# Unit 0 of a fused gated-recurrence and feed-forward kernel: stacking issued from two queues, its four score groups ahead of its outputs, its transposes and state updates last

## The chip, the cores and the metric

The kernel runs on one core of a Trainium2 chip. The metric is the time of one execution in device microseconds (us), as the median of the runs shown: 691.08 us over three runs (691.05 to 691.49).

## What is computed

The reference runs a gated linear recurrence over the sequence and feeds its output to a feed-forward layer. There are 4 batches, 8 heads, 768 tokens and 48 values to a head; the state is a complex 48x48 matrix for each batch and head.

```python
mag = np.sqrt(a_re * a_re + a_im * a_im)
scale = np.minimum(mag, 0.999) / (mag + 1e-06)
...
for t in range(S):
    new_re = ar * S_re - ai * S_im
    new_im = ar * S_im + ai * S_re
    S_re, S_im = (new_re + kv, new_im)          # kv = outer(k_t, v_t)
    y[:, :, t] = np.einsum('bhd,bhde->bhe', q[:, :, t], S_re)
...
x = attn_out.transpose(0, 2, 1, 3).reshape(B * S, H * D)   # 3072 x 384
return ((x @ w_a) * (x @ w_b)) @ w_out                     # d_ff = 1536
```

## The kernel before

**Units.** The work is cut into 12 units: 2 pairs of batches by 6 chunks of 128 tokens. A unit has 256 columns (its two batches, i = 0 and 1). The recurrence over a chunk is turned into products of matrices: with the cumulative products of the gates, z, multiplied into q and divided out of k, the output of a chunk is a masked score matrix times v plus q times the state that came in, and the state is carried from chunk to chunk.

**Steps of a unit u.**

- prep(u), on DVE (VectorE) and ACT (ScalarE): the gates are normed (L178 to L193), the cumulative products are built (L211 and L213, then pairs of L227 and L233, then L289, L294, L297 to L305), and q and k are multiplied by them. The last two operations of prep(u) are the two multiplications L309 into the tile qk.
- stack(u), L338 to L347: ten DMAs from SBUF to SBUF bring the eight heads of qk into the tile stk, each head on partitions of its own. Two heads straddle a block of partitions and take two DMAs each. SP (SyncE) issues all of them in before. There is one stk and one qk, so the next load of q and k waits for the whole of stack.
- attn(u): scores(i, g), with g one of two groups of four heads: four matmuls into a tile pm on PE (TensorE, L379), then the multiplication by the causal mask into a tile am on DVE (L382). There are two am buffers. outputs(i): 16 matmuls of am and v into xp, and 16 more of q and the state except where a chunk begins a sequence (L422), then ACT casts xp to xh (L424). residual(i): xp minus xh, by a matmul with a negated identity on PE (L432) and a cast on ACT (L435) for units 0 and 1, on DVE for later units. transposes(i, g): four on PE (L390) and a copy to kt on ACT (L394). state(i, g): four matmuls of kt and v (L445), and then a copy into the state u on ACT where a chunk begins a sequence (L454) or an addition on DVE (L452).
- the feed-forward of unit u (its window): for each of 12 blocks f of the inner dimension gemm1 (L489, 18 matmuls), a copy h_t on ACT (L497), the product h_t on DVE (L498), a cast hh on ACT (L499), a difference hl on DVE (L500), and gemm2 (L507, six matmuls) two blocks later. After each unit its output is stored from ACT's queue (L647).

The matmuls work on pairs of a rounded number and its remainder, so the weights are split once at the start (split_weights): per piece three operations on DVE (L134, L136, L138), a cast (L142) and a copy (L149) on ACT, and two matmuls (L147, L148). Six blocks of the weights are split ahead of unit 0's attention, the others during window 0. A weight piece is called w, then m (0, 1 or 2: w_a, w_b, w_out), then f: w111 is w_b's block 11.

**What sets the order.** The program is written as one stream of steps. Unit 0's attention stands in front of window 0, with parts of prep(1) between its steps; the attention of unit w+1 is put between the blocks f of window w, and stack(w+2) and the load behind it follow at a fixed block of window w. Within a step, priorities move the DVE and ACT operations of attention and feed-forward ahead (ATTN_FIRST, MOE_FIRST), and a scheduler that runs when the program is built puts each engine's instructions into one fixed order. On the chip each engine then works its own list in that order and waits on semaphores. The pools that tie the engines: three buffers for ab (gemm1's output), two for pm, one for xp, two for am, two for kt.

**Unit 0's order** (L463 to L466) is a list of its own: the scores of batch 0, its outputs, the scores of batch 1, the residual of batch 0, outputs of batch 1, transposes of batch 0, and then the rest. The list of later units stands above it.

Of the kernel before, what the change touches and what calls it, by code (L numbers as in the profile page):

```python
# [8 lines left out]
F32 = mybir.dt.float32  # L9
# [58 lines left out]
def tile_kernel(ctx: ExitStack, tc: tile.TileContext, a_d, qk_d, v_d, w_d, qn_d, kn_d, vn_d, an_d, out_d):  # L68
    nc = tc.nc
    vec, act, pe, sync = nc.vector, nc.scalar, nc.tensor, nc.sync  # L70
# [8 lines left out]
    kvp = fast.enter_context(tc.tile_pool(name="kvp", bufs=2))  # L79
# [26 lines left out]
    stk = const.tile([128, H, RUN], F32, name="stk")  # L106
    nc.gpsimd.memset(stk[KS:128], 0.0)
    qk = const.tile([128, NJ, 2, RUN], F32, name="qk")
# [88 lines left out]
    def rescaled(c):  # L197
        return c % 2 == 1 and c + 1 < NCH
# [139 lines left out]
    def stack(u):  # L338
        n = RUN if rescaled(u % NCH) else 2 * TOK
        for h in range(H):  # L340
            r0 = h * D
            while r0 < (h + 1) * D:
                j, p = divmod(r0, 128)
                m = min((h + 1) * D - r0, 128 - p)
                d0 = 2 * (r0 - h * D)
                sync.dma_start(out=stk[d0:d0 + 2 * m, h, 0:n], in_=qk[p:p + m, j, :, 0:n])
                r0 += m  # L347


# [12 lines left out]
                          (3 * g + 2, [(2 * g, 32), (2 * g + 1, 64)])):  # L362
            quads[q % 4].append((q // 4, [(h, g * 128 + off) for h, off in pieces]))

    def attn(u, xh, xl):

        c = u % NCH
        last = c + 1 == NCH
# [2 lines left out]
        def cols(i):  # L371
            return slice(i * C, (i + 1) * C), slice(TOK + i * C, TOK + (i + 1) * C)

        def scores(i, hg):
            qs, ks = cols(i)
            sp = ps_m.tile([128, 4, 128], F32, name="pm")
            for h4 in range(4):
                h = hg * 4 + h4
                pe.matmul(out=sp[:, h4], lhsT=stk[:, h, ks], rhs=stk[:, h, qs], start=True, stop=True)  # L379
            am = kvp.tile([128, 512], F32, name="am", bufs=2).rearrange("p (h t) -> p h t", h=4)  # L380
            with tc.high_priority(offset=ATTN_FIRST):
                vec.tensor_tensor(out=am, in0=sp, in1=mask[:].unsqueeze(1).broadcast_to([128, 4, 128]),  # L382
                                  op=ALU.mult)
            ams[i, hg] = am
# [52 lines left out]
        def state(i, hg):  # L437
# [12 lines left out]
            with tc.high_priority(offset=ATTN_FIRST):  # L450
# [4 lines left out]
                if rescaled(c):  # L455
                    vec.tensor_tensor(out=uv, in0=uv, in1=sv, op=ALU.mult)

        order = [(scores, 0, 0), (scores, 0, 1), (transposes, 0, 0), (transposes, 0, 1),
                 (outputs, 0, 0), (scores, 1, 0), (residual, 0, 0), (state, 0, 0), (scores, 1, 1),
                 (state, 0, 1), (transposes, 1, 0), (transposes, 1, 1), (outputs, 1, 0),  # L460
                 (state, 1, 0), (residual, 1, 0), (state, 1, 1)]
        if u == 0:
            order = [(scores, 0, 0), (scores, 0, 1), (outputs, 0, 0), (scores, 1, 0), (scores, 1, 1),  # L463
                     (residual, 0, 0), (outputs, 1, 0), (transposes, 0, 0), (transposes, 0, 1),
                     (residual, 1, 0), (state, 0, 0), (state, 0, 1), (transposes, 1, 0), (transposes, 1, 1),
                     (state, 1, 0), (state, 1, 1)]  # L466
        for fn, i, g in order:
            if not (last and fn in (transposes, state)):
                fn(i, g)
# [5 lines left out]
    def new_x():  # L475
        return (moe.tile([128, NJ, TOK], F32, name="xh"), moe.tile([128, NJ, TOK], F32, name="xl"))
# [139 lines left out]
    def drain(gen, ns=None):  # L616
        if gen is None:
            return
        left = ns
        for cost in gen:  # L620
            if left is not None:
                left -= cost or 0
                if left <= 0:
                    return
# [6 lines left out]
    p1 = prep(1)  # L631
    for _ in range(CONV_FIRST):
        next(ws)
    x_cur = new_x()
    for _ in attn(0, *x_cur):
        drain(p1, P1_A)
    pend = []

# [11 lines left out]
    for w in range(NU):  # L650
# [42 lines left out]
        x_cur = x_nxt  # L693
# [74 lines left out]
```

## Time and profile before

| what | value |
|---|---|
| median of 3 runs | 691.08 us (691.05 to 691.49) |
| the profiled execution: its time | 690.18 us |
| its span on the core | 688.5 us |
| instructions in it | 14290 |
| mean granted clock of PE | 0.972 |
| HBM read, written | 39.32 MB, 4.72 MB |

The profile is one execution of its own; its time lies 0.9 us below the median, and 1.7 us of it lie outside the span. All start times below are microseconds from the span's start. A row of a timeline has the start, the time from the first start to the last end of the instructions in it, the engine, the line, the operation and its tiles, how many there are, and in brackets how long the engine stood idle before it and what ended that. Instructions overlap in an engine's pipeline, so the distance from one start to the next is what an instruction adds.

### The profile page before, as it was taken

To read this page: it belongs to the slowest core of one execution; us is meant where nothing else is said; L and a number is where in the kernel's file an instruction comes from. 1 tells how busy PE (TensorE), PEld (TensorE's weight loads), DVE (VectorE), ACT (ScalarE), POOL (GpSimd) and SP (SyncE) were. 2 spreads that over 40 slices of the span, in tenths; PEclk is the share of its full clock that TensorE was granted. 3 is DMA by queue.
4 is the path that set the end of the run, shared out by engine and by line. 5 is a ranking of instruction groups with operands and counts; after the bars stand their busy time and mean duration, and the time that the engine had idled before them with its cause. 6 is when DMAs were issued, how large, how long until landed. Compare 5 with 4: busy or idle time off the path is not lost.

```text
span 688.5 us, 14290 instructions
## 1 busy us (share of the span) xinstructions
PE 644.5 (94%) x5842; PEld 608.3 (88%) x5842; DVE 550.1 (80%) x1259; ACT 310.1 (45%) x622; POOL 5.6 (1%) x11
## 2 busy tenths in 40 slices
PE   3547999999999999999999999999999999999996
PEld 1214889899999999999999999999999999999996
DVE  6999899998989989999898898999989963233221
ACT  7357664735445346354363553635542332221221
POOL 3000000000000000000000000000000000000000
PEclk9676999999999999999999999999999999999999
DMA  8963301513314225043160440611500500400000
GB/s 321 402 268 95 121 1 44 143 54 87 115 39 139 63 78 145 16 136 104 29 194 2 122 117 3 178 60 62 155 24 18 153 24 18 108 24 2 24 1 28
DMA packets 30232, 63.94 MB, mean 93 GB/s; under 512 B 3664, under 2 KB 7248, under 8 KB 30160
## 3 DMA queue, kind: packets, MB, share of 16 engines
q1 hardware_dynamic: 26704, 58.23, 27.3%
q10 hardware_dynamic: 3456, 4.72, 1.9%
q8 instruction: 48, 0.79, 0.5%
q14 instruction: 24, 0.20, 0.1%
HBM read 39.32 MB, written 4.72 MB: 64 GB/s over the span
## 4 chain that ended last, share of the span: by engine, by line
PE 66%; DVE 25%; ACT 4%; DMA 2%; issue 2%; SPq 0%; DVEq 0%; ACTq 0%
PE ab L489 33%; PE o L507 16%; PE xp L422 5%; PE pm L379 4%; PE pm L445 3%; DVE a_t L289 3%; DVE qk L309 2%; PE pm L390 2%; DVE h_t L498 2%; DVE hl L500 2%; PE pm L147 1%; DVE z L294 1%; DVE pr L227 1%; DVE am L382 1%; DVE pb L262 1%
## 5 line engine op out<-in xcount | busy, mean ns | idle before, releaser
L489 PE MATMUL ab<-xh,w 128*128 128x256 f32 x1728 | 341.6, 286 | 0.0
L489 PEld LDWEIGHTS ab<-xh,w 128*128 128x128 f32 x1728 | 277.2, 189 | 1.7 <-issue 0.8
L489 PE MATMUL ab<-xl,w 128*128 128x256 f32 x864 | 245.5, 284 | 0.0
L489 PEld LDWEIGHTS ab<-xl,w 128*128 128x128 f32 x864 | 163.0, 189 | 0.6 <-issue 0.2
L507 PE MATMUL o<-w,hh 128*128 128x384 f32 x576 | 152.7, 343 | 0.0
L497 ACT COPY h_t<-ab 128x256 f32<-128x256 f32 x144 | 53.4, 371 | 163.4 <-PE ab L489 163.4
L498 DVE TENSOR_TENSOR h_t<-ab,h_t 128x256 f32<-128x256 f32 x144 | 60.4, 420 | 64.6 <-ACT h_t L497 64.3
L507 PEld LDWEIGHTS o<-w,hh 128*128 128x128 f32 x576 | 96.6, 188 | 1.1 <-issue 1.0
L507 PE MATMUL o<-w,hl 128*128 128x384 f32 x288 | 97.2, 338 | 0.0
L499 ACT CAST hh<-h_t 128x256 fp32r<-128x256 f32 x144 | 58.0, 403 | 78.0 <-DVE h_t L498 76.9
L500 DVE TENSOR_TENSOR hl<-h_t,hh 128x256 fp32r<-128x256 f32 x144 | 60.4, 419 | 16.6 <-ACT hh L499 16.4
L379 PE MATMUL pm<-stk 128*128 128x128 f32 x384 | 54.8, 280 | 2.1 <-DMA stk<-qk 2.0
L147 PE MATMUL ab<-o_sb,ident 128*128 128x384 f32 x42 | 28.1, 764 | 29.7 <-DVE o_sb L138 29.7
L379 PEld LDWEIGHTS pm<-stk 128*128 128x128 f32 x384 | 50.2, 194 | 5.7 <-issue 3.6
L507 PEld LDWEIGHTS o<-w,hl 128*128 128x128 f32 x288 | 54.1, 188 | 0.0
L227 DVE TENSOR_TENSOR pr<-z 128x384 f32<-128x384 f32 (+1 forms) x91 | 47.2, 525 | 1.8
L289 DVE TENSOR_TENSOR a_t<-z,b_t 128x768 f32<-128x768 f32 x48 | 44.7, 947 | 0.1
L147 PEld LDWEIGHTS ab<-o_sb,ident 128*128 128x128 f32 x42 | 9.5, 268 | 39.3 <-DVE o_sb L138 30.3
L309 DVE TENSOR_TENSOR qk<-qk,z 128x1536 f32<-128x1536 f32 (+1 forms) x26 | 42.3, 1626 | 0.2
L422 PE MATMUL xp<-am,v_t 128*32 128x128 f32 x768 | 37.7, 281 | 4.3 <-DVE am L382 4.1
L382 DVE TENSOR_TENSOR am<-pm,mask 128x512 f32<-128x512 f32 x48 | 32.7, 685 | 5.2 <-PE pm L379 4.4
L424 ACT CAST xh<-xp 128x384 fp32r<-128x384 f32 x24 | 11.4, 475 | 49.3 <-PE xp L422 49.1
(107 smaller groups left out, 768.7 us busy)
## 6 DMA issues: line engine op xcount, KB each, us to landing
w<-in_dram SPq DMA_DIRECT2D x36, 384.0 KB, 8.0
qk<-in_dram SPq DMA_DIRECT2D x12, 768.0 KB, 4.9
stk<-qk SPq DMA_DIRECT2D x48, 192.0 KB, 3.3
a_t<-in_dram SPq DMA_DIRECT2D x11, 768.0 KB, 4.3
v_t<-in_dram SPq DMA_DIRECT2D x24, 256.0 KB, 2.7
stk<-qk SPq DMA_DIRECT2D x24, 192.8 KB, 3.3
out_dram<-o_sb ACTq DMA_DIRECT2D x24, 192.0 KB, 1.9
stk<-qk SPq DMA_DIRECT2D x16, 128.0 KB, 3.1
```

The source lines that it names most:

```text
L147: pe.matmul(out=lp[:, 0:n], lhsT=ident, rhs=t, start=True, stop=False)
L227: vec.tensor_tensor(out=pr[:, :, :, o:o + n], in0=view(zz, W + at_(i) + 2 * o, [[W, 2], [-W, 2], [2, n]]), in1=tok(slice(1, 3), i - 1, o, ...
L289: vec.tensor_tensor(out=pz[:, s].rearrange("p (j b e) -> p j b e", j=SUB // 2, e=2), in0=zb[:, 1 + s], in1=view(bb, (1 + k - s) * NB, [[0, ...
L309: vec.tensor_tensor(out=qk4[:, :, k, x0:x1], in0=qk4[:, :, 1, x0:x1], in1=z[:, k].rearrange("p (j t) -> p j t", j=NJ).unsqueeze(2).broadca ...
L379: pe.matmul(out=sp[:, h4], lhsT=stk[:, h, ks], rhs=stk[:, h, qs], start=True, stop=True)
L422: run = pe.matmul(out=xp[qd * 32:(qd + 1) * 32, ti], lhsT=l, rhs=rr, start=st, stop=sp_, tile_position=(0, qd * 32), skip_group_check=True ...
L489: pe.matmul(out=ab[:, m * TOK:(m + 1) * TOK], lhsT=r(w_ab(f, part, m * NJ + i)), rhs=r(xt[:, i, :]), start=n == 0, stop=n == 8)
L497: act.copy(out=h_t, in_=ab[:, 0:TOK])
L498: vec.tensor_tensor(out=h_t, in0=ab[:, TOK:2 * TOK], in1=h_t, op=ALU.mult)
L499: act.copy(out=r(hh), in_=h_t)
L500: vec.tensor_tensor(out=r(hl), in0=h_t, in1=hh, op=ALU.subtract)
L507: pe.matmul(out=os_[tt][:, 0:DM], lhsT=r(ht[:, ts]), rhs=r(w_t[f, 2][:, part, :]), start=(f == 0 and n == 0), stop=(f == NF - 1 and n == 2))
```

## The change

1. In stack(0), the DMAs of the odd heads are issued by ACT's queue, five of ten; SP keeps the five of the even heads. Later units are stacked by SP alone, as before.
2. Unit 0's attention is written in another order: all four score groups, outputs and residual of batch 0, outputs and residual of batch 1, then transposes and states of batch 0, then those of batch 1.
3. The masked scores of batch 1 of unit 0 go to two tiles of the size of xh and xl, which the pool has for a later unit, in place of the two am buffers. So the four masked score tiles of unit 0 have four places.

```diff
@@ stack
-                sync.dma_start(out=stk[d0:d0 + 2 * m, h, 0:n], in_=qk[p:p + m, j, :, 0:n])
+                eng = act if u == 0 and h % 2 else sync
+                eng.dma_start(out=stk[d0:d0 + 2 * m, h, 0:n], in_=qk[p:p + m, j, :, 0:n])
@@ attn
-    def attn(u, xh, xl):
+    def attn(u, xh, xl, spare={}):
...
-            am = kvp.tile([128, 512], F32, name="am", bufs=2).rearrange("p (h t) -> p h t", h=4)
+            if (i, hg) in spare:
+                am = spare[i, hg].rearrange("p j t -> p (j t)")[:, 0:512].rearrange("p (h t) -> p h t", h=4)
+            else:
+                am = kvp.tile([128, 512], F32, name="am", bufs=2).rearrange("p (h t) -> p h t", h=4)
...
         if u == 0:
-            order = [(scores, 0, 0), (scores, 0, 1), (outputs, 0, 0), (scores, 1, 0), (scores, 1, 1),
-                     (residual, 0, 0), (outputs, 1, 0), (transposes, 0, 0), (transposes, 0, 1),
-                     (residual, 1, 0), (state, 0, 0), (state, 0, 1), (transposes, 1, 0), (transposes, 1, 1),
-                     (state, 1, 0), (state, 1, 1)]
+            order = [(scores, 0, 0), (scores, 0, 1), (scores, 1, 0), (scores, 1, 1),
+                     (outputs, 0, 0), (residual, 0, 0), (outputs, 1, 0), (residual, 1, 0),
+                     (transposes, 0, 0), (transposes, 0, 1), (state, 0, 0), (state, 0, 1),
+                     (transposes, 1, 0), (transposes, 1, 1), (state, 1, 0), (state, 1, 1)]
@@ the main program
+    am_first = new_x()
     x_cur = new_x()
-    for _ in attn(0, *x_cur):
+    for _ in attn(0, *x_cur, {(1, 0): am_first[0], (1, 1): am_first[1]}):
         drain(p1, P1_A)
```

The lines below L346 move by one, and those below L380 by four: scores are L380 after, the mask L386, transposes L394, kt L398, outputs L426, their cast L428, residual L436 and L439, state L449 and L458, gemm1 L493, h_t L502, hl L504, gemm2 L511.

The scheduler places the instructions of the rest of the program around the new list. Three places are shown, each by what stands on an engine before and after.

PE, from unit 0's scores on (w_747 and the like are lower parts of weights that are being split, o_sb their whole numbers). Before:

```order
L148 MATMUL ab<-w_757,nident 128x384
L379 MATMUL pm<-stk 128x128 x2
L148 MATMUL ab<-w_767,nident 128x384
L379 MATMUL pm<-stk 128x128 x7
L422 MATMUL xp<-am,v_t 32x128 x16
L379 MATMUL pm<-stk 128x128 x4
L432 MATMUL xp<-xh,nident 128x384
L390 MATMUL pm<-ident,stk 128x96 x4
L422 MATMUL xp<-am,v_t 32x128 x16
L390 MATMUL pm<-ident,stk 128x96 x4
L445 MATMUL pm<-v_t,kt 96x96 x4
L432 MATMUL xp<-xh,nident 128x384
```

After:

```order
L380 MATMUL pm<-stk 128x128 x2
L147 MATMUL ab<-o_sb,ident 128x384
L380 MATMUL pm<-stk 128x128 x8
L148 MATMUL ab<-w_747,nident 128x384
L148 MATMUL ab<-w_757,nident 128x384
L426 MATMUL xp<-am,v_t 32x128 x16
L380 MATMUL pm<-stk 128x128 x4
L394 MATMUL pm<-ident,stk 128x96 x4
L436 MATMUL xp<-xh,nident 128x384
L148 MATMUL ab<-w_767,nident 128x384
L394 MATMUL pm<-ident,stk 128x96 x4
L426 MATMUL xp<-xl,v_t 32x128 x6
```

The third score group now stands ahead of the first outputs, and the L148 matmuls of three weight pieces come later, behind the first three score groups or the first residual; the masked scores of batch 1 are called xh and xl, after the tiles they lie in.

On ACT, the five DMAs of the odd heads stand between the copy of the weight w_506 (L149) and L180 of prep(1); L187 of prep(1) moves from ahead of unit 0's first cast xh to behind its kt copy and its cast xl, and L213 of prep(1) from behind the first kt copy to behind three of the four copies into the state.

DVE, up to the second L309 of prep(1), behind which stack(1) stands (h_t and hl with their numbers are feed-forward blocks of window 0, o_sb_1078 and o_sb_1088 the pieces w111 and w211 of the weights). Before:

```order
L309 TENSOR_TENSOR qk_110<-qk_110,z_577 128x3x512
L498 TENSOR_TENSOR h_t_1291<-ab_1272,h_t_1291 128x256
L309 TENSOR_TENSOR qk_110<-qk_110,z_577 128x3x512
L500 TENSOR_TENSOR hl_1293<-h_t_1291,hh_1292 128x256
L498 TENSOR_TENSOR h_t_1337<-ab_1318,h_t_1337 128x256
L138 SCALAR_TENSOR_TENSOR o_sb_1078<-w111_196,o_sb_1078 128x384
L134 TENSOR_SCALAR o_sb_1088<-w211_198 128x384
L500 TENSOR_TENSOR hl_1339<-h_t_1337,hh_1338 128x256
L136 SCALAR_TENSOR_TENSOR o_sb_1088<-w211_198,o_sb_1088 128x384
L211 TENSOR_TENSOR z_1478<-a_t_575,sc_618 128x96x4x2
L138 SCALAR_TENSOR_TENSOR o_sb_1088<-w211_198,o_sb_1088 128x384
L498 TENSOR_TENSOR h_t_1383<-ab_1364,h_t_1383 128x256
```

After:

```order
L136 SCALAR_TENSOR_TENSOR o_sb_1078<-w111_196,o_sb_1078 128x384
L134 TENSOR_SCALAR o_sb_1088<-w211_198 128x384
L318 TENSOR_TENSOR a_t_144<-a_t_144 128x768
L138 SCALAR_TENSOR_TENSOR o_sb_1078<-w111_196,o_sb_1078 128x384
L502 TENSOR_TENSOR h_t_1337<-ab_1318,h_t_1337 128x256
L320 SCALAR_TENSOR_TENSOR a_t_144<-a_t_144 128x768
L504 TENSOR_TENSOR hl_1339<-h_t_1337,hh_1338 128x256
L324 TENSOR_TENSOR qk_110<-qk_110,a_t_144 128x3x256
L136 SCALAR_TENSOR_TENSOR o_sb_1088<-w211_198,o_sb_1088 128x384
L309 TENSOR_TENSOR qk_110<-qk_110,z_577 128x3x512
L502 TENSOR_TENSOR h_t_1383<-ab_1364,h_t_1383 128x256
L309 TENSOR_TENSOR qk_110<-qk_110,z_577 128x3x512
```

Seven operations that stood behind the second L309 now stand ahead of it: hl_1293 (four rows above this piece), h_t_1337, hl_1339, h_t_1383, L138 of w111, and L134 and L136 of w211. On PE, 18 matmuls of gemm1 and 14 of gemm2 and one L148 have likewise moved from behind unit 1's first score matmul to ahead of it.

PE, at unit 2's first score matmul in window 1 (w17, w08 and w18 are gemm1's weights, w25 and w26 gemm2's). Before:

```order
L507 MATMUL o0_1588<-w25_506,hh_1861 128x384 x2
L507 MATMUL o0_1588<-w25_506,hl_1862 128x384
L507 MATMUL o1_1589<-w25_506,hh_1861 128x384 x2
L507 MATMUL o1_1589<-w25_506,hl_1862 128x384
L489 MATMUL ab_2030<-xh_735,w08_873 128x256
L489 MATMUL ab_2030<-xl_736,w08_873 128x256
L489 MATMUL ab_2030<-xh_735,w08_873 128x256 x2
L489 MATMUL ab_2030<-xl_736,w08_873 128x256
L489 MATMUL ab_2030<-xh_735,w08_873 128x256 x2
L489 MATMUL ab_2030<-xl_736,w08_873 128x256
L489 MATMUL ab_2030<-xh_735,w08_873 128x256
L379 MATMUL pm_1908<-stk_108 128x128
```

After:

```order
L493 MATMUL ab_1947<-xh_735,w17_825 128x256 x2
L493 MATMUL ab_1947<-xl_736,w17_825 128x256
L380 MATMUL pm_1908<-stk_108 128x128
L493 MATMUL ab_1947<-xh_735,w17_825 128x256
L511 MATMUL o0_1588<-w25_506,hh_1861 128x384 x2
L511 MATMUL o0_1588<-w25_506,hl_1862 128x384
L380 MATMUL pm_1908<-stk_108 128x128
L511 MATMUL o1_1589<-w25_506,hh_1861 128x384 x2
L511 MATMUL o1_1589<-w25_506,hl_1862 128x384
L493 MATMUL ab_2030<-xh_735,w08_873 128x256
```

The first score matmul has moved up past the last matmul of w17, the six of w25 and the nine of w08: ten of gemm1 and six of gemm2 that stood ahead of it stand behind it. On DVE one h_t and one hl have moved from ahead of prep(2)'s second L309 to behind it. From unit 3 on, as many instructions stand ahead of a unit's scores and its stack as before.

## The prediction

> **What bounds the kernel now.** The page comes first: the span, and the busy time of the two engines that are near it.
>
> ```profile
> span 688.5 us, 14290 instructions
> PE 644.5 (94%) x5842; PEld 608.3 (88%) x5842; DVE 550.1 (80%) x1259; ACT 310.1 (45%) x622; POOL 5.6 (1%) x11
> ```
>
> PE bounds the whole, but that is an average. The change acts at the start, so I cut the first third into stretches: unit 0's attention, up to the last multiplication of prep(1), up to that of prep(2), the wait for unit 2's stack, and up to that of prep(3). The columns behind the length are PE, PEld, DVE, ACT and POOL busy with their counts, then granted clock, DMA share, GB/s.
>
> ```profile
> 57.60:76.09 18.49, 13.71 (x119) 10.45 (x120) 16.14 (x29) 11.61 (x21) 0.00 (x0) 0.76 0.56 164
> 76.09:121.18 45.09, 45.07 (x306) 40.19 (x305) 44.73 (x110) 29.03 (x64) 0.00 (x0) 1.00 0.10 33
> 121.18:167.62 46.44, 46.30 (x454) 44.05 (x453) 42.09 (x95) 23.22 (x45) 0.00 (x0) 1.00 0.31 89
> 167.62:171.12 3.50, 2.13 (x17) 1.96 (x15) 3.46 (x7) 2.58 (x4) 0.00 (x0) 1.00 0.55 143
> 171.12:213.63 42.51, 42.51 (x436) 41.79 (x437) 37.81 (x87) 19.29 (x40) 0.00 (x0) 1.00 0.27 86
> ```
>
> In the first stretch PE stands idle for 18.49 - 13.71 = 4.78 us and runs at 0.76 of its clock. From 76 to 121 PE and DVE are both full (DVE idle 0.36 us of 45.09). From 171 to 214 PE has no idle time at all. The waits of PE from 76 to 680 (total, times, longest) say the same of the rest:
>
> ```profile
> PE pm L379 <- DMA stk<-qk: 2.0, 2, 1.4
> PE xp L422 <- DVE am L382: 1.6, 3, 0.8
> ```
>
> So a microsecond that PE saves in unit 0 is worth one only if DVE, which is just as full up to 121, moves up too.
>
> **Unit 0: what goes.** The rows of PE there:
>
> ```profile
> 65.84 1.72 PE L379 MATMUL pm<-stk 128*128 128x128 f32 x14
> 69.79 1.93 PE L422 MATMUL xp<-am,v_t 128*32 128x128 f32 x32 [2.22 <-DVE am L382]
> ...
> 74.40 1.08 PE L422 MATMUL xp<-am,v_t 128*32 128x128 f32 x32 [0.36 <-DVE am L382]
> ...
> 81.89 0.81 PE L147 MATMUL pm<-o_sb,ident 128*128 128x384 f32 x2
> ```
>
> and the granted clock behind the idle 2.22 us, with the DMA share (the last but one column) while the stack is in flight:
>
> ```profile
> 69.79:73.30 3.51, 3.51 (x41) 3.03 (x41) 2.37 (x3) 0.48 (x1) 0.00 (x0) 0.52 0.41 159
> 58.60:66.60 8.00, 6.33 (x26) 4.52 (x27) 7.20 (x16) 7.08 (x13) 0.00 (x0) 0.73 0.75 198
> ```
>
> The first outputs wait 2.22 us for a masked tile, and then PE runs 3.51 us at 0.52. The Trainium skill ("TensorE: Matmul & The Clock Gate", "What's actually happening") has the clock fall after an idle window of about 3.4 us; here 2.22 us of idle time were enough, so the row decides. With more scores ahead of the outputs this gap closes.
>
> How fast the stack becomes: SP issues ten DMAs, an ACT DMA issue takes 338 ns, and a stack DMA lands some 3.3 us after its issue:
>
> ```profile
> 57.63 6.81 SPq L346 DMA_DIRECT2D stk<-qk  x10
> ```
>
> ```profile
> L647 ACTq DMA_DIRECT2D out_dram<-o_sb x22: 338/338/417, 149.6 to 649.0; - x22
> ```
>
> ```profile
> stk<-qk SPq DMA_DIRECT2D x24, 192.8 KB, 3.3
> ```
>
> ```profile
> 58.10 0.48 ACT L149 CAST w<-ab 128x384 fp32r<-128x384 f32 x1 [0.78 <-PE ab L148]
> 58.50 0.94 ACT L180 ACTIVATE sc<-a_t,biases 128x768 f32<-128x768 f32 x1
> ...
> 63.84 0.85 ACT L184 ACTIVATE a_t<-sc 128x768 f32<-128x768 f32 x1
> ...
> 75.15 0.84 ACT L213 ACTIVATE z<-z 128x768 f32<-128x768 f32 x1 [0.55 <-DVE z L211]
> ```
>
> ACT's five stand behind its L149, so they begin near 58.5; the fifth of a queue waits for the landing of its first (they share a semaphore), near 61.6, and is out by 62.2. The last head then lands near 65.3. The bounds: 8.0 us at 0.75 are 6.0 us of all 16 DMA engines, so not ahead of 58.6 + 6.0 = 64.6; and not behind today's 66.4 or so, when the scores of 65.84 run to their end. I take 65.3 and the first scores done by 66.1. What is queued behind: ACT's L180 to L184 slip by 3.7 us (58.50 to 62.2; between 0 if they issue at once and 4.7), so L184 ends near 68.65 instead of 64.7, and L213 now stands behind the state copies.
>
> PE in the new order: outputs of batch 0 from 66.45 instead of 69.79, at full clock. The masks of batch 1 wait for DVE's L186, which waits for L184: 68.65 + 0.95 + 0.65 = 70.25. The outputs of batch 1 run at 70.45 instead of 74.40. The rest of unit 0 and of block 0 then takes as long as before, so gemm1 of block 0 ends at 77.65 instead of 81.89: **PE leads by 4.2 us.**
>
> DVE gains nothing of that. Its rows:
>
> ```profile
> 76.09 0.56 DVE L227 TENSOR_TENSOR pr<-z 128x384 f32<-128x384 f32 x1
> ```
>
> Its first mask comes earlier, but L189 and L211 hang on ACT's late L184 and L187 (L211 from 74.4 to 76.1), and L227 on the late L213: 76.55 instead of 76.09. **DVE lags by 0.46 us**; the bounds are -2.35 (all the idle time of that stretch gone, 18.49 - 16.14) and +2.0 (stack no faster).
>
> **Where the order moves.** The last multiplication of prep(1), behind which stack(1) stands, and what follows it now:
>
> ```profile
> 119.43 1.75 DVE L309 TENSOR_TENSOR qk<-qk,z 128x1536 f32<-128x1536 f32 x1
> 121.10 0.42 DVE L500 TENSOR_TENSOR hl<-h_t,hh 128x256 fp32r<-128x256 f32 x1
> 121.43 0.41 DVE L498 TENSOR_TENSOR h_t<-ab,h_t 128x256 f32<-128x256 f32 x1
> 121.77 0.55 DVE L138 SCALAR_TENSOR_TENSOR o_sb<-w,o_sb 128x384 uint32<-128x384 uint32 x1
> 122.23 0.35 DVE L134 TENSOR_SCALAR o_sb<-w 128x384 uint32<-128x384 uint32 x1
> 122.50 0.42 DVE L500 TENSOR_TENSOR hl<-h_t,hh 128x256 fp32r<-128x256 f32 x1
> 122.84 0.55 DVE L136 SCALAR_TENSOR_TENSOR o_sb<-w,o_sb 128x384 uint32<-128x384 uint32 x1
> 123.31 0.95 DVE L211 TENSOR_TENSOR z<-a_t,sc 128x768 f32<-128x768 f32 x1
> ```
>
> From start to start: hl 0.33, h_t 0.34, L138 0.46, L134 0.27, L136 0.47. The seven operations that now precede it add 2 x 0.34 + 2 x 0.33 + 0.46 + 0.27 + 0.47 = 2.54 us. With the lag it ends at 121.18 + 0.46 + 2.54 = 124.2 (call this T1). The stretch before is full on DVE, so nothing hides this. On PE, 18 matmuls of gemm1, 14 of gemm2 and one L148 move ahead of unit 1's scores. Their price (critical chain, undisturbed):
>
> ```profile
> 92.81 2.13 PE ab L489 x18
> 94.94 1.05 PE o L507 x6
> ...
> 97.45 0.17 PE pm L148
> ```
>
> 2.13 + 14/6 x 1.05 + 0.17 = 4.75 us: the lead is spent there, and afterwards PE has that much less to do between unit 1's steps, each of which waits for a mask from DVE. PE starves there, by about the same 4.75 us in sum.
>
> Unit 1's last mask and window 1's first gemm1 before, and the next two marks:
>
> ```profile
> 138.97 0.68 DVE L382 TENSOR_TENSOR am<-pm,mask 128x512 f32<-128x512 f32 x1
> ```
>
> ```profile
> 142.77 0.28 PE L489 MATMUL ab<-xh,w 128*128 128x256 f32 x1
> ...
> 171.12 0.46 PE L379 MATMUL pm<-stk 128*128 128x128 f32 x2 [1.37 <-DMA stk<-qk]
> ```
>
> ```profile
> 165.87 1.75 DVE L309 TENSOR_TENSOR qk<-qk,z 128x1536 f32<-128x1536 f32 x1
> ```
>
> The mask came 17.8 us after T1; I take the same, so window 1 starts at 142.77 + 3.0 = 145.8, less some 0.2 for matmuls between the masks: 145.6. PE's own way to unit 2's scores was 171.12 - 1.37 - 142.77 = 26.98 us; it now has ten of gemm1 and six of gemm2 less on it, 10/18 x 2.13 + 1.05 = 2.23 us. So PE arrives at 145.6 + 24.75 = 170.35. DVE from T1 to the last L309 of prep(2): 46.44 before, less the 2.54 already done, less one h_t and one hl that now come behind, 0.67: 43.2, if its idle time (46.44 - 42.09 = 4.35) stays. That ends at 124.2 + 43.2 = 167.4 to 167.5, and unit 2's scores start 3.50 us later, as before, at 171.0. That is 0.1 earlier than before, but with 2.23 us of work still to do that was done before. From there to unit 3's stack nothing is idle, and from unit 3 on the order of steps is as before. **Sum: 171.0 - 171.12 + 2.23 = +2.1 us.** If DVE's idle time went, PE's arrival would set it: 170.35 - 171.12 + 2.23 = +1.5; if DVE's prep(2) met 0.8 us more of waiting, +2.9. The spare mask tiles cost nothing: no transfer or instruction is added.
>
> The profiled execution's span of 688.5 becomes 690.6 and its time 690.18 becomes 692.3; the median lies 0.9 above, so 691.08 + 2.1 = 693.2, and this case spans 692.5 to 694.0.
>
> **The rivals.** A (faster): DVE does not lag. If its 2.35 us of idle time in the first stretch goes, and the 0.36 behind it, T1 is 121.18 - 2.71 + 2.54 = 121.0, window 1 starts 3.2 us earlier than in my sum, and PE's arrival gives 1.5 - 3.2 = -1.7: 689.4, or 688.8 if the wait at unit 3's stack goes as well:
>
> ```profile
> 217.14 0.46 PE L379 MATMUL pm<-stk 128*128 128x128 f32 x2 [0.65 <-DMA stk<-qk]
> ```
>
> It decides from T1 at 121.3 or earlier. For it: masks come 3 us earlier and SP's queue is half as long. Against it: L213 behind the state copies, and L184 behind five DMA issues.
>
> B (no change): half of that idle time goes, T1 is near 122.8, and the sum is between 1.5 - 1.4 and 2.1 - 1.4: 691.2 to 691.8.
>
> C (slower still, the stack does not do what the edit says): the DMA engines were already 0.75 busy, and the last landing stays at its place while ACT has lost 3.7 us. DVE lags by 2.0 instead of 0.46, and the sum is 2.1 + 1.5 = +3.6: 694.7. The Trainium skill says so too ("DMA: Bandwidth & Descriptors", "Issuing engines are not separate DMA queues"): several issuing engines share the same 16 engines and save only issue time. The trace can't settle it, since SP's own issues fill 6.81 us.
>
> D (clock): PE, starving at unit 1's masks, falls to half clock as behind 69.79, where 3.51 us at 0.52 cost 1.7. In front of window 1 that adds up to 1.7: 694.9. Against it: the idle 1.37 us ahead of 171.12 left the clock at 1.00 in both stretches beside it, and the new gaps are split by masks.
>
> **How the numbers follow.** My forecast 0.44, A 0.22, B 0.20, C 0.09, D 0.05. A measurement of this kernel can tell about 0.2%, 1.4 us, from no change: 689.7 to 692.5. My case lies above it except at its edge (0.05 of its 0.44 below), A below it, B within. Faster 0.22, same 0.25, slower 0.53. The range reaches from 688.8 (most of A) to 695.4 (C and D with half a microsecond).
>
> **What would show it.** Right: gemm1 of block 0 over by about 77.7, no gap of 2 us ahead of unit 0's first outputs, prep(1)'s last L309 ending near 124.2, some 5 us of PE waits for masks between 126 and 146, prep(2)'s near 167.5, unit 2's first scores near 171.0 with 16 matmuls fewer behind PE. Wrong: T1 at 122 or less (A, B), the stack landing no earlier than before (C), a granted clock under 0.9 between 126 and 150 (D), or a new wait of PE behind unit 3, where I count none.

## The result, and the profile after

The changed kernel takes 696.46 us (median of 4 runs, 694.36 to 697.17) against 691.07 us before (4 runs beside it, 690.79 to 691.49): a ratio of 1.0073, 95% interval 1.005 to 1.0095. It is slower, as forecast, but by 5.4 us in place of 2.1, and outside the range, which ended at 695.4. The profiled execution took 694.36 us, the fastest of the four, 4.2 us over the profiled one of before.

The page of the changed kernel: PE's busy time rises by 2.9 us with the same count of instructions, DVE's hardly at all, and the span by 4.1 us.

```profile
span 692.6 us, 14279 instructions
...
PE 647.4 (93%) x5842; PEld 608.7 (88%) x5842; DVE 550.4 (79%) x1259; ACT 310.1 (45%) x622; POOL 5.6 (1%) x11
```

The same stretches as in the prediction, each from its own first mark: prep(0)'s last L309 (58.73, before 57.53), the first L227 of prep(1), the end of prep(1)'s last L309 (called T1), that of prep(2), unit 2's first score, and the end of prep(3). The first mark lies 0.07 us ahead of the end that the row of this L309 shows, in every trace alike; "behind prep(0)" is counted from it. The prediction's first stretch began at the end itself, 57.60, and so has 18.49 us where 18.56 is counted here.

```profile
58.73:78.96 20.23, 18.36 (x166) 13.94 (x167) 16.47 (x29) 13.58 (x29) 0.00 (x0) 0.83 0.51 141
78.96:126.09 47.13, 46.87 (x306) 41.60 (x305) 46.83 (x117) 28.63 (x61) 0.00 (x0) 1.00 0.11 36
126.09:169.99 43.90, 40.23 (x389) 37.04 (x388) 39.44 (x87) 21.27 (x39) 0.00 (x0) 0.96 0.32 94
169.99:173.48 3.49, 2.18 (x18) 2.00 (x18) 3.35 (x7) 1.98 (x3) 0.00 (x0) 1.00 0.57 149
173.48:217.20 43.72, 43.72 (x446) 43.01 (x447) 38.37 (x89) 20.47 (x41) 0.00 (x0) 1.00 0.27 83
```

Unit 0 takes 20.23 us in place of 18.56, the stretch to T1 47.13 in place of 45.09, and DVE is full in the second of them (46.83). From T1 to prep(2) it is 43.90 in place of 46.44, and PE stands idle for 3.67 us there, where it had stood for 0.14. The waits of PE from 76 to 680 show by their releasers what was added (the prediction has two rows of before, 2.0 and 1.6 us):

```profile
PE pm L380 <- DMA stk<-qk: 3.2, 5, 1.3
PE xp L426 <- DVE am L386: 2.2, 4, 0.8
PE pm L394 <- DVE am L386: 0.7, 2, 0.5
PE pm L380 <- ACT kt L398: 0.6, 1, 0.6
```

In unit 0, DVE's rows (first mask, L186, first L227, prep(1)'s last L309):

```profile
66.10 0.69 DVE L386 TENSOR_TENSOR am<-pm,mask 128x512 f32<-128x512 f32 x1 [2.95 <-PE pm L380]
...
71.28 0.96 DVE L186 TENSOR_TENSOR a_t<-a_t 128x768 f32<-128x768 f32 x1 [0.38 <-ACT a_t L184]
...
78.96 0.56 DVE L227 TENSOR_TENSOR pr<-z 128x384 f32<-128x384 f32 x1 [0.15 <-ACT z L213]
...
124.34 1.75 DVE L309 TENSOR_TENSOR qk<-qk,z 128x1536 f32<-128x1536 f32 x1
```

and the first mask of before:

```profile
64.91 0.69 DVE L382 TENSOR_TENSOR am<-pm,mask 128x512 f32<-128x512 f32 x1
```

The first mask comes 66.10 - 58.73 = 7.37 us behind prep(0)'s last L309; before it was 64.91 - 57.53 = 7.38. Two queues brought it not one tenth sooner, and DVE, whose fixed list has the mask behind eight operations after prep(1)'s L179 in place of 13, stands in front of it for 2.95 us. Before, it did not wait there. On ACT the five issues hold L180 until 64.09, and a later L149 waits 1.50 us for PE:

```profile
59.38 4.66 ACTq L347 DMA_DIRECT2D stk<-qk  x5
64.09 0.93 ACT L180 ACTIVATE sc<-a_t,biases 128x768 f32<-128x768 f32 x1 [4.29 <-DMA stk<-qk]
...
68.91 0.48 ACT L149 CAST w<-ab 128x384 fp32r<-128x384 f32 x1 [1.50 <-PE ab L148]
```

How the stack lands is told by its DMAs (how many, their size, median us to landing; the six of the whole heads stand for all ten) and by SP's next load of q and k, which waits for all ten. Before:

```profile
stk<-qk SPq DMA_DIRECT2D x6, 192.0 KB, 3.1
```

```profile
67.23 0.60 SPq L336 DMA_DIRECT2D qk<-in_dram  x1
```

After:

```profile
stk<-qk SPq DMA_DIRECT2D x3, 192.0 KB, 4.5
stk<-qk ACTq DMA_DIRECT2D x3, 192.0 KB, 4.1
```

```profile
58.84 4.56 SPq L347 DMA_DIRECT2D stk<-qk  x5
67.63 0.60 SPq L336 DMA_DIRECT2D qk<-in_dram  x1
```

By that load the whole stack is in 8.90 us behind prep(0) in place of 9.70, but the median DMA of 192 KB takes 4.1 to 4.5 us in place of 3.1. Taken one by one (the trace infers which landing belongs to which issue), the first four heads, which the first mask needs, are in 6.2 us behind prep(0), before 6.0: they come no sooner.

### The profile page after: what moved, and what is told of

It reads as the page before. It is cut to its first block, busy times and chain, and to the rows that moved or that the text cites. A ratio compares the mean times of both kernels' runs of the same rounds, so it can differ in the third digit from the quotient of the medians.

```text
span 692.6 us, 14279 instructions
## 1 busy us (share of the span) xinstructions
PE 647.4 (93%) x5842; PEld 608.7 (88%) x5842; DVE 550.4 (79%) x1259; ACT 310.1 (45%) x622; POOL 5.6 (1%) x11
## 4 chain that ended last, share of the span: by engine, by line
PE 66%; DVE 24%; ACT 4%; DMA 3%; issue 2%; SPq 1%; DVEq 0%; ACTq 0%
PE ab L493 33%; PE o L511 16%; PE xp L426 5%; PE pm L380 5%; PE pm L449 3%; DVE a_t L289 3%; PE pm L394 2%; DVE qk L309 2%; DVE h_t L502 2%; DVE hl L504 1%; DVE z L294 1%; DVE pb L262 1%; DMA a_t<-in_dram 1%; DVE o_sb L136 1%; DVE b_t L268 1%
## 5 line engine op out<-in xcount | busy, mean ns | idle before, releaser
L493 PE MATMUL ab<-xh,w 128*128 128x256 f32 x1728 | 338.8, 285 | 0.0
L493 PEld LDWEIGHTS ab<-xh,w 128*128 128x128 f32 x1728 | 276.6, 189 | 1.1 <-issue 0.6
L493 PE MATMUL ab<-xl,w 128*128 128x256 f32 x864 | 245.5, 284 | 0.0
L493 PEld LDWEIGHTS ab<-xl,w 128*128 128x128 f32 x864 | 163.0, 189 | 0.5 <-issue 0.2
L511 PE MATMUL o<-w,hh 128*128 128x384 f32 x576 | 152.5, 344 | 0.0
L502 DVE TENSOR_TENSOR h_t<-ab,h_t 128x256 f32<-128x256 f32 x144 | 60.6, 421 | 64.5 <-ACT h_t L501 64.3
L511 PEld LDWEIGHTS o<-w,hh 128*128 128x128 f32 x576 | 96.5, 188 | 1.2 <-issue 0.8
L511 PE MATMUL o<-w,hl 128*128 128x384 f32 x288 | 97.4, 339 | 0.0
L504 DVE TENSOR_TENSOR hl<-h_t,hh 128x256 fp32r<-128x256 f32 x144 | 60.5, 420 | 15.7 <-ACT hh L503 15.6
L380 PE MATMUL pm<-stk 128*128 128x128 f32 x384 | 55.9, 283 | 3.8 <-DMA stk<-qk 3.2
L380 PEld LDWEIGHTS pm<-stk 128*128 128x128 f32 x384 | 49.8, 193 | 8.9 <-issue 4.4
L147 PE MATMUL ab<-o_sb,ident 128*128 128x384 f32 x42 | 28.5, 778 | 30.8 <-DVE o_sb L138 30.8
L511 PEld LDWEIGHTS o<-w,hl 128*128 128x128 f32 x288 | 54.1, 188 | 0.5 <-issue 0.2
L227 DVE TENSOR_TENSOR pr<-z 128x384 f32<-128x384 f32 (+1 forms) x91 | 47.2, 525 | 2.3 <-ACT z L213 0.5
L147 PEld LDWEIGHTS ab<-o_sb,ident 128*128 128x128 f32 x42 | 9.6, 274 | 40.4 <-DVE o_sb L138 29.9
L309 DVE TENSOR_TENSOR qk<-qk,z 128x1536 f32<-128x1536 f32 (+1 forms) x26 | 42.3, 1628 | 0.1
L426 PE MATMUL xp<-am,v_t 128*32 128x128 f32 x736 | 36.6, 280 | 2.3 <-DVE am L386 2.2
L386 DVE TENSOR_TENSOR am<-pm,mask 128x512 f32<-128x512 f32 x46 | 31.3, 685 | 7.3 <-PE pm L380 7.3
L449 PEld LDWEIGHTS pm<-v_t,kt 128*96 128x96 f32 x320 | 32.4, 164 | 0.9 <-issue 0.4
```

The lines of the kernel that those rows point to most:

```text
L227: vec.tensor_tensor(out=pr[:, :, :, o:o + n], in0=view(zz, W + at_(i) + 2 * o, [[W, 2], [-W, 2], [2, n]]), in1=tok(slice(1, 3), i - 1, o, ...
L309: vec.tensor_tensor(out=qk4[:, :, k, x0:x1], in0=qk4[:, :, 1, x0:x1], in1=z[:, k].rearrange("p (j t) -> p j t", j=NJ).unsqueeze(2).broadca ...
L426: run = pe.matmul(out=xp[qd * 32:(qd + 1) * 32, ti], lhsT=l, rhs=rr, start=st, stop=sp_, tile_position=(0, qd * 32), skip_group_check=True ...
L449: pe.matmul(out=kp[0:KS, h4 * n:(h4 + 1) * n], lhsT=kts[i, hg][:, h4, :], rhs=v_t[:, o:o + n], start=True, stop=True)
L493: pe.matmul(out=ab[:, m * TOK:(m + 1) * TOK], lhsT=r(w_ab(f, part, m * NJ + i)), rhs=r(xt[:, i, :]), start=n == 0, stop=n == 8)
L502: vec.tensor_tensor(out=h_t, in0=ab[:, TOK:2 * TOK], in1=h_t, op=ALU.mult)
```

## The experiments

Two theories stood at the start. Q: the loss comes from the second queue, by what it holds up and by what the scheduler makes of it. O: it comes from the new order of unit 0, which spends PE's work early and lets PE starve at unit 1. All runs are the whole computation. The first four runs take the change apart.

**One part alone.** x1_two_queues is the kernel before with the first edit only:

```diff
-                sync.dma_start(out=stk[d0:d0 + 2 * m, h, 0:n], in_=qk[p:p + m, j, :, 0:n])
+                eng = act if u == 0 and h % 2 else sync
+                eng.dma_start(out=stk[d0:d0 + 2 * m, h, 0:n], in_=qk[p:p + m, j, :, 0:n])
```

> The kernel before with the first edit alone: unit 0's odd heads are stacked by ACT's queue, order and mask tiles as before. Theory Q (the queue is the cause: ACT is held by its five issues, prep(1) is late on DVE, and with other instructions ready the scheduler puts six more ahead of prep(1)'s last L309): nearly all of the loss is here, 694 to 697 us, prep(1)'s last L309 ends 3.5 to 5 us later than before's 121.2, and ACT's L180 starts near 64 in place of 58.5. Theory O (the new order of unit 0 is the cause, through PE starving at unit 1): 690.5 to 692 us, last L309 within 1 us of before.

Measured: 696.06 us, ratio 1.0073 (1.0059 to 1.0086), the whole loss. The first mask and prep(1)'s last L309:

```profile
66.41 0.69 DVE L383 TENSOR_TENSOR am<-pm,mask 128x512 f32<-128x512 f32 x1 [3.36 <-PE pm L380]
```

```profile
126.20 1.75 DVE L309 TENSOR_TENSOR qk<-qk,z 128x1536 f32<-128x1536 f32 x1
```

A wait of the same kind at the mask, and T1 at 127.95, 6.8 us later than before where 3.5 to 5 were expected. Theory Q holds, with a later T1 than it gave.

x2_order_spare_sp is the changed kernel without that edit:

```diff
-                eng = act if u == 0 and h % 2 else sync
+                eng = sync
```

> The changed kernel with the first edit taken back: SP issues all ten stack DMAs, the new order and the spare mask tiles stay. One instruction fewer than before stands ahead of prep(1)'s last L309 on DVE (9 h_t, 9 hl, 34 of each weight operation, in place of 9, 8, 35, 35 and 34). Theory Q: not slower than before, 688.5 to 691 us, last L309 at 119.5 to 121.5. Theory O: 694 to 696.5 us, as the changed kernel.

Measured: 689.34 us, ratio 0.9977 (0.9967 to 0.9987): faster than before. Its first mask waits 0.26 us, and though prep(0) ended late in this execution (59.31), T1 is at 121.21:

```profile
66.97 0.69 DVE L386 TENSOR_TENSOR am<-pm,mask 128x512 f32<-128x512 f32 x1 [0.26 <-PE pm L380]
```

```profile
119.46 1.75 DVE L309 TENSOR_TENSOR qk<-qk,z 128x1536 f32<-128x1536 f32 x1
```

Theory O falls: the order with its tiles is a gain of 1.6 us, and the second queue turns it into a loss.

x3_order_no_spare takes the spare mask tiles away as well:

```diff
-    am_first = new_x()
...
-    for _ in attn(0, *x_cur, {(1, 0): am_first[0], (1, 1): am_first[1]}):
+    for _ in attn(0, *x_cur):
```

> As the run with the new order and SP's stack, and the spare mask tiles taken back too: batch 1's masks wait for am buffers that outputs of batch 0 must read first. On DVE as many instructions as before stand ahead of prep(1)'s last L309. If the spare tiles matter, batch 1's first mask comes some 1 us later than with them and the time is 0.5 to 1.5 us longer; if PE's lead is worth nothing because DVE sets unit 1, within 0.3 us of it. Theory Q: 688.5 to 691.5 us either way. Theory O: 694 or more.

Measured: 690.93 us, ratio 1.0 (0.9991 to 1.0009). Without the tiles the new order is worth nothing. The tiles without the order weren't tried.

x4_pool_queue gives the odd heads to GpSimd's queue, so that ACT isn't held:

```diff
-                eng = act if u == 0 and h % 2 else sync
+                eng = nc.gpsimd if u == 0 and h % 2 else sync
```

> The changed kernel with the odd heads issued by GpSimd's queue in place of ACT's: ACT is not held, but seven more instructions still stand ahead of prep(1)'s last L309 on DVE. Theory Q in two parts: without the hold of ACT (L180 back near 58.5 to 59.5) the lag at unit 0's end goes, some 1.7 us, and the reordering stays, some 2.5 us: 692.5 to 694.5 us. If the hold alone is the cause: 690 to 691.5. If the DMA engines are the limit, the stack's last heads land as late as in the changed kernel, 7.5 us or more behind the first issue.

Measured: 693.58 us, ratio 1.0041 (1.0029 to 1.0054). L180 is back at 59.81, and DVE still stands 3.82 us in front of the first mask. The loss is smaller, but not gone with the hold of ACT.

**The reordering alone.** x5_order_repaired keeps the change and ties the instructions that had moved ahead of prep(1)'s last L309 behind it again:

```diff
+    def behind(cond):
+        return tc.issue_after(last_p[1]) if cond and win[0] == 0 and 1 in last_p else ExitStack()
...
-            vec.tensor_tensor(out=h_t, in0=ab[:, TOK:2 * TOK], in1=h_t, op=ALU.mult)
+            with behind(f > 8):
+                vec.tensor_tensor(out=h_t, in0=ab[:, TOK:2 * TOK], in1=h_t, op=ALU.mult)
...
-            vec.tensor_tensor(out=r(hl), in0=h_t, in1=hh, op=ALU.subtract)
+            with behind(f > 7):
+                vec.tensor_tensor(out=r(hl), in0=h_t, in1=hh, op=ALU.subtract)
```

and L134 and L136 of w211 and L138 of w111 and w211 in the same way; last_p holds the last L309 of each prep, win the window.

> The changed kernel as it is, with ACT's five issues, but eight DVE instructions of window 0 tied behind prep(1)'s last L309 (h_t from block 9 on, hl from block 8 on, the last operations of w111 and w211), so that 278 instructions stand ahead of it as against 286 in the changed kernel and 279 before. If hold and reordering are two separate prices: the reordering's 2 to 2.5 us goes and unit 0's lag on DVE of 1.7 us stays: 692 to 693.5 us, prep(1)'s last L309 64.5 to 65.5 us behind that of prep(0) (63.7 before, 67.4 in the changed kernel), no PE idle time above 2 us in sum between it and window 1. If the hold of ACT alone is the cause, and the order only follows it: 695 us or more. If the reordering alone is: 690.5 to 691.5.

Measured: 693.86 us, ratio 1.0046 (1.0025 to 1.0067), beside 696.65 for the changed kernel on the same chip: 2.8 us of the loss were the reordering. The time lies just above the 692 to 693.5 us that were expected, with DVE idle for 5.30 us.

x6_pool_order_repaired puts the tie and GpSimd's queue together.

> The same tie with the odd heads on GpSimd's queue: neither ACT's hold nor the reordering. Two prices: both gone, 690 to 691.8 us, within 0.2% of before, because DVE's lag at unit 0's end was only 0.4 us there. If more queues on the DMA engines cost by themselves (last heads landing later than by SP alone), 692 or more.

Measured: 693.23 us, ratio 1.0032 (1.0017 to 1.0046). Not back at the time before. ACT's hold and the added work are gone, but the mask still stands ten operations behind L179, and DVE waits 3.74 us there; so this doesn't yet show what a second queue costs by itself. In x4_pool_queue the stack DMAs land in 5.4 to 6.9 us (medians by size and queue), and here the first mask comes 8.98 us behind prep(0).

x7_changed_again is the changed kernel once more.

> The changed kernel once more, for the spread of its times and a second trace. 694 to 697.5 us. If its spread comes from PE's clock in the sparse stretch at unit 1, this trace too has a granted clock under 1.00 there, at another place or of another length than the 0.77 that the first trace shows from 134 to 140. If it comes from the preamble, the distance from prep(0)'s last L309 to the end is the same as in the first trace within 0.5 us (692.6 - 58.7 = 633.9).

Measured: 696.65 us (696.01 to 697.52), ratio 1.007 (1.005 to 1.0091). From prep(0)'s last L309 to the end it took 637.3 us, 3.4 more than in the first trace; so the difference between these two traces isn't the preamble's. What differs is told below.

**What makes DVE stand idle.** x8_two_heads_on_act leaves two heads on ACT:

```diff
-                eng = act if u == 0 and h % 2 else sync
+                eng = act if u == 0 and h in (1, 3) else sync
```

> The changed kernel with only heads 1 and 3 on ACT's queue: two issues there, none of which waits for a landing, eight on SP. Four more instructions than before stand ahead of prep(1)'s last L309 in place of seven. Two prices in between: ACT's L180 near 60 (1.5 us of hold), 691.5 to 693.5 us. If any use of ACT's queue costs the whole, 695 or more; if stacking is faster with two queues when ACT isn't held, 689.5 or less.

Measured: 693.98 us, ratio 1.0036 (1.0024 to 1.0048). L180 is at 60.33, hardly held, and DVE is idle for 3.39 us at the first mask and 1.03 at another. The 691.5 to 693.5 us that were expected from a shorter hold are missed.

x9_changed_warm, x10_order_spare_warm and x11_before_warm ask whether PE's clock does it. The traces had shown half clock for some 5 to 6 us behind prep(0) with one queue and longer with two. Idle matmuls, whose result nobody reads, keep PE busy just ahead of the stack:

```diff
+        idle = ps_m.tile([128, 512], F32, name="pm")
...
+                if f in (4, 5):
+                    for _ in range(4):
+                        with tc.issue_after(run):
+                            run = pe.matmul(out=idle[:, 0:n], lhsT=r(nident), rhs=r(hi), start=True, stop=True).ins
```

> The changed kernel with four idle matmuls (the result is never read) behind each of the six L148 of weight blocks 4 and 5, just ahead of the stack; the order of all other instructions is as in the changed kernel. In the traces so far PE comes to full clock 5.2 to 5.6 us behind the last L309 of prep(0) where SP stacks alone, and 6.4 to 10.6 us behind it where two queues do. If the late clock makes unit 0's lag: full clock at the stack, prep(1)'s first L227 within 19 us of prep(0)'s last L309 (20.2 and 21.9 in the changed kernel, 18.6 before), and 693 to 694.8 us, since the reordering ahead of prep(1)'s last L309 stays. If the hold of ACT makes it: L227 still at 20 or more, 695.5 to 697 us.

Measured: 695.82 us, ratio 1.007 (1.0058 to 1.0082), and the first mask:

```profile
65.58 0.69 DVE L391 TENSOR_TENSOR am<-pm,mask 128x512 f32<-128x512 f32 x1 [4.03 <-PE pm L385]
```

PE entered the stack at full clock, and unit 0 was no shorter (its L227 21.28 us behind prep(0)). Some 2 us into the stack the clock fell back to half all the same, in a stretch in which PE was busy for 3.21 of 5.00 us, so this doesn't show what a clock that stays would give; a full clock at the start alone didn't help here.

> The same idle matmuls in the kernel with SP's stack, the new order and the spare tiles. Clock theory: unit 0 a little faster still, 688 to 689.3 us. Hold theory, or the clock being early enough there already: 689 to 690, no difference from the run without them. If idle matmuls get in the way of the weights' own (0.17 to 0.35 us each), over 690.5.

Measured: 689.5 us, ratio 0.9978 (0.9967 to 0.9989); no difference from x2_order_spare_sp in the median. In its one trace the clock stayed at 1.00 from the stack on, and the first mask came 6.83 us behind prep(0), against 7.66 in the trace of x2_order_spare_sp, at half clock up to 6.0.

> The same idle matmuls in the kernel before. The half-clock stretch of 3.5 us behind the first outputs' wait comes 14 us later and isn't touched by them. Clock theory: full clock at the stack, but unit 0 waits for the stack and DVE: 690 to 691.3 us. If PE's clock there bounds unit 0, 689.5 or less.

Measured: 690.58 us, ratio 0.9992 (0.9983 to 1.0001); within what can be told from no change.

x12_last_heads_on_act keeps ACT's two issues, but for heads 6 and 7 (`h > 5` in the same line). The scheduler then puts the first mask behind 13 operations, as before.

> As the run with heads 1 and 3 on ACT, but heads 6 and 7 are the two on ACT's queue. ACT's list is the same up to L183; the difference is that the first mask (L386) stands behind 13 operations on DVE after prep(1)'s L179, as before, in place of ten. Five more instructions than before (four in the other run) stand ahead of prep(1)'s last L309. If DVE's standing at a mask that the scheduler put too early makes the idle time: idle time of DVE from prep(0)'s last L309 to prep(1)'s near 2.7 us (6.0 in the other run, 2.7 before), and with five more instructions, some 1.7 us, 691.8 to 693 us. If the second queue or ACT's two issues make it wherever the mask stands: idle 4.5 or more, 693.5 to 694.5 us.

Measured: 693.13 us, ratio 1.0032 (1.002 to 1.0044). DVE is idle for 4.19 us in all, between the two expectations; at the first mask 1.78.

x13_last_heads_order_repaired adds the tie to it.

> The same two heads on ACT, and the tie that keeps eight instructions of window 0 behind prep(1)'s last L309. Both prices gone if they are these two: 60.9 us or less of DVE work and 3 us or less of idle time between the two last L309, 689.5 to 691.3 us, not slower than before with two queues. If a second queue costs by itself, 692 or more.

Measured: 692.29 us, ratio 1.0019 (1.0011 to 1.0028). With the mask in its old place, DVE's work as before and ACT's L180 (here L189) started only 1.3 us later behind prep(0), 1.2 us stay: this is what a second queue with two issues costs where the order is repaired, and it is an expectation missed. The first four heads, all from SP here, are in 8.5 us behind prep(0) in place of 6.0, and DVE waits 1.55 us for the first mask.

x14_second_group_on_act gives ACT heads 4 to 7 (`h > 3`): ACT held, the mask later.

> Heads 4 to 7 (five issues, so that ACT is held as in the changed kernel) on ACT, heads 0 to 3 on SP; the first two masks stand side by side behind 11 operations on DVE (eight in the changed kernel, 13 before); five more instructions ahead of prep(1)'s last L309. If ACT's hold makes DVE idle even with the mask later: L180 near 5.3 us behind prep(0)'s last L309, DVE idle 4 to 6 us, 693.5 to 696 us. If only the mask's place does: idle 3 to 4, 692.5 to 694.

Measured: 694.95 us, ratio 1.0062 (1.0044 to 1.008). DVE stands for 2.35 us in front of an L134 that needs ACT's cast L142, and again 2.35 us at the masks. So the hold is a price too: what stands next in DVE's list waits, for the mask or for ACT.

**All runs in one table.** From the end of prep(0)'s last L309 to T1, with DVE's busy time in it and the rest idle, and from T1 to the end of the span (each from its own profiled execution):

| kernel | to T1 | DVE busy | DVE idle | first mask behind prep(0) | T1 to end |
|---|---|---|---|---|---|
| before | 63.65 | 60.95 | 2.70 | 7.38 | 567.3 |
| x3: order, no spare tiles | 63.58 | 60.92 | 2.66 | 7.32 | 566.9 |
| x11: before, idle matmuls | 63.95 | 60.88 | 3.07 | 7.66 | 567.9 |
| x2: order and spare tiles | 61.90 | 60.40 | 1.50 | 7.66 | 566.9 |
| x10: the same, idle matmuls | 61.08 | 60.20 | 0.88 | 6.83 | 567.5 |
| changed | 67.36 | 63.30 | 4.06 | 7.37 | 566.5 |
| x7: changed again | 69.14 | 63.48 | 5.66 | 8.23 | 568.1 |
| x9: changed, idle matmuls | 68.80 | 63.32 | 5.48 | 8.45 | 567.3 |
| x1: two queues only | 69.31 | 63.20 | 6.11 | 7.77 | 566.6 |
| x5: changed, order repaired | 66.57 | 61.27 | 5.30 | 7.72 | 567.8 |
| x8: heads 1, 3 on ACT | 68.06 | 62.06 | 6.00 | 8.63 | 566.5 |
| x12: heads 6, 7 on ACT | 66.84 | 62.65 | 4.19 | 9.47 | 566.3 |
| x13: x12, order repaired | 65.23 | 61.15 | 4.08 | 9.15 | 566.7 |
| x14: heads 4 to 7 on ACT | 68.18 | 62.47 | 5.71 | 10.05 | 566.7 |
| x4: odd heads on GpSimd | 67.01 | 62.77 | 4.24 | 9.15 | 567.1 |
| x6: x4, order repaired | 65.26 | 60.51 | 4.75 | 8.98 | 567.8 |

Three of its rows as the windows have them (DVE's busy time and count stand behind PE's and PEld's), first of before, then the changed kernel, then x2_order_spare_sp:

```profile
57.53:121.18 63.65, 58.85 (x422) 50.71 (x423) 60.95 (x139) 40.64 (x84) 0.00 (x0) 0.93 0.23 71
```

```profile
58.73:126.09 67.36, 65.22 (x469) 55.54 (x470) 63.30 (x146) 42.21 (x89) 0.00 (x0) 0.95 0.23 67
```

```profile
59.31:121.21 61.90, 58.14 (x424) 50.16 (x425) 60.40 (x138) 40.73 (x84) 0.00 (x0) 0.95 0.24 73
```

Behind T1 every kernel needs 566.3 to 568.1 us, while the way to T1 differs by up to 8.2. So the larger part of the differences lies ahead of T1, and that way is DVE's work plus DVE's idle time. The instructions that are moved ahead of the last L309 are the work (146 in place of 139); the standing, most of it in unit 0, is the idle time. Each row is one execution, and the two of the changed kernel differ by 1.8 us, so small differences between rows say little.

## Why the prediction was wrong in its size

**Which step failed.** The step "Unit 0: what goes", where the stack's last head was to land near 65.3 and the first scores to be done by 66.1, and from which DVE's lag of 0.46 us followed. Its last head landed 8.7 us behind prep(0), forecast 7.8; before it was 9.5, where I had read 8.9 off the scores. So as a whole the stack did come sooner (by 0.8 us, forecast 1.1), but not the four heads that the first mask needs: they were in 6.2 us behind prep(0) in the first trace and 5.9 in the second, with one queue 6.0, and the first mask came at 7.37 and 8.23, before at 7.38. I had the landing of 3.3 us from a row in which one queue issued alone, and kept it for two; it was 4.1 to 4.6. And I had its first mask earlier and no wait of DVE in front of it, where its list now has the mask eight operations behind L179 and it stands there for 2.95 and 3.82 us. ACT's hold was under-sized too: L180 started 5.36 us behind prep(0), forecast 4.6, and L183 and L184 then waited for an L149 whose matmul L148 now stands behind scores. The lag at the first L227 came to 20.23 - 18.56 = 1.67 us in one trace and 3.3 in the other, in place of 0.46.

The bounds that I had set for that lag, -2.35 to +2.0, held the first trace and not the second. Of the rivals' numbers, those of C, no faster stack, and D, the clock, came nearest with 694.7 and 694.9, and both were too low. C's lag of 2.0 us lay between the two traces' 1.67 and 3.3, though the last landing did not stay at its place but came 0.8 us sooner. I gave C 0.09. The Trainium skill ("DMA: Bandwidth & Descriptors", "Issuing engines are not separate DMA queues") says that several issuing engines save only the time of issuing. The trace agrees: the last issue was out 1.6 us sooner behind prep(0) (by the rows of the issues, 59.38 + 4.66 - 58.73 = 5.31 in place of 57.63 + 6.81 - 57.53 = 6.91), and the stack was in only 0.8 us sooner.

Two small sums of the same step don't close: L184's end of 64.7, late by 3.7, gives 68.4 and not 68.65, and outputs of batch 1 that start 3.95 us sooner give gemm1's end at 77.94 and not 77.65. The second doesn't enter the +2.1; the first can have made the lag too large, by 0.25 us at most.

**What held.** The reordering on DVE was forecast at 2.54 us; the busy time rose by 2.35 and 2.53 us in the two traces, and taking it away gave 2.8 us back. What was to come behind T1, 2.1 - 3.0 = -0.9 us, came out at -0.8 in the first trace and +0.8 in the second; that the first fits is in part luck, since the kernels here differ by 1.8 us behind T1. PE starved at unit 1 by 3.67 us in the first trace, forecast 4.75, but masks released only 0.9 us of it; unit 1's stack released 3.2 - 1.3 = 1.9. PE's wait at unit 2's scores is there at its place, with 3.49 us behind prep(2) as before:

```profile
173.48 0.46 PE L380 MATMUL pm<-stk 128*128 128x128 f32 x2 [1.32 <-DMA stk<-qk]
```

The gap of 2.2 us ahead of the first outputs went, as forecast, and no half clock followed it. PE's lead over before, 4.2 us by forecast, was 81.89 - 80.02 = 1.9 by start times and 3.1 from prep(0) on.

**The sum, term by term.** First trace against before: prep(0) ended 1.2 us later, which lies in the spread of the traces without idle matmuls (57.5 to 59.6, ahead of all that their edits touch); DVE idle +1.36; DVE work +2.35; behind T1 -0.8; together 4.1. Second trace: 0.9 + 2.96 + 2.53 + 0.8 = 7.2.

**Rival D** was more than its 0.05: in the starved stretch at unit 1 the granted clock fell. The third figure from the right of each row is the clock; first the changed kernel, then its second trace, then x5_order_repaired.

```profile
134.00:140.00 6.00, 4.39 (x50) 3.40 (x52) 5.72 (x13) 4.37 (x7) 0.00 (x0) 0.77 0.47 151
140.00:146.00 6.00, 5.41 (x92) 4.92 (x84) 4.98 (x11) 1.10 (x3) 0.00 (x0) 0.95 0.21 60
```

```profile
134.00:140.00 6.00, 4.77 (x24) 2.92 (x27) 5.49 (x13) 5.04 (x7) 0.00 (x0) 0.74 0.57 152
140.00:146.00 6.00, 6.00 (x86) 5.28 (x86) 4.33 (x11) 1.90 (x3) 0.00 (x0) 0.70 0.37 128
```

```profile
134.00:140.00 6.00, 4.53 (x73) 4.10 (x75) 5.76 (x13) 4.87 (x8) 0.00 (x0) 1.00 0.52 158
140.00:146.00 6.00, 5.08 (x88) 4.58 (x84) 5.83 (x13) 2.53 (x4) 0.00 (x0) 1.00 0.21 71
```

From T1 to window 1's first gemm1 it took 22.1 and 22.9 us in the two traces with the lower clock, and 21.8 in the third; before it was 21.6. It costs at most 1.3 us, and where in the stretch it falls changes from run to run.

The clock differs in unit 0 too: it is back at 1.00 from 6.8 us behind prep(0) in the first trace and from 10.1 in the second. With the first four heads in at 5.9, PE in the second trace doesn't stand idle again before the first mask (66.67), but works at half clock, with an L147 of the weights between the second head and the last two of the group:

```profile
63.64 0.79 PE L380 MATMUL pm<-stk 128*128 128x128 f32 x2 [0.67 <-DMA stk<-qk]
64.23 1.49 PE L147 MATMUL ab<-o_sb,ident 128*128 128x384 f32 x2
65.51 1.06 PE L380 MATMUL pm<-stk 128*128 128x128 f32 x4
```

```profile
62.90:67.50 4.60, 3.93 (x11) 2.79 (x11) 0.83 (x2) 3.25 (x5) 0.00 (x0) 0.50 0.78 193
```

The second fence is the stretch around these rows, with the clock at 0.50. So part of the standing at the mask is PE's clock, and not the landing. That the spread of the changed kernel's times comes from the clock at these two places is read from two traces; it wasn't tried by itself.

**What stays open.** How the added idle time divides between the mask's early place, ACT's hold, the second queue's slower landings and PE's half clock in the changed kernel itself: x8, x12, x13 and x14 show that the first three make DVE wait, not how they add, and no run held the clock at 1.00 with two queues. A kernel with two queues and the list of one queue wasn't tried.

**A version that beats both:** SP's stack, the new order and the spare tiles, 689.34 us, 0.23% under before (0.13 to 0.33%).

## What to carry to other kernels

When an engine with a full list bounds a stage, add up its work and its idle time to the point that the next stage waits for: here 3.7 us in one trace came from 2.4 of work put ahead and 1.4 of standing, 5.5 in another from 2.5 and 3.0, and what came behind that point moved by 0.8 us at most. Two issuing queues shortened this stack by 0.8 us only; ask when the first piece lands that somebody waits for, not when the last does. And an edit to a queue must be read in the fixed order of the other engines too: here the scheduler put the waiting mask behind eight operations in place of 13. That it did so because it takes the transfer of two queues for faster than it is fits x12_last_heads_on_act, where the mask kept its place, but wasn't shown.

## What the runs showed of the hardware that was not expected

Stack DMAs took 3.1 us (192 KB, median) from one queue, 4.1 to 4.5 from SP and ACT together in the changed kernel's first trace, and 5.4 to 6.3 from SP and GpSimd together in x4_pool_queue, where five issues kept GpSimd busy for 2.80 us. The granted clock rose to 1.00 between 5.3 and 6.0 us behind prep(0) in the three traces with one queue and no idle matmuls, and for good not ahead of 6.8 us in those with two, apart from x13_last_heads_order_repaired (5.3). Idle matmuls ahead of the stack kept it at 1.00 through the stack in x10_order_spare_warm alone: in x9_changed_warm it went back to half within the stack, after some 7 us at full clock, and in x11_before_warm 2.6 us behind prep(0). At unit 1 it fell to 0.50 at 137.2 us in the changed kernel's first trace and at 136.8 in the second, though from T1 up to there PE had not stood idle for more than 0.70 us at a time.
